# A fused scan, mixture-of-experts and Fourier-mixing kernel: the last scatters are freed from the early rows' load, and three small steps change place

## The chip, the cores and the metric

The kernel runs on one core of a Trainium2 chip. The metric is the device time of one execution in microseconds, the median of several runs. Each run is one program on one core.

## The reference

```python
# 1. attention-like scan: batch 4, heads 8, length 768, head size 32, state 16
state = decay_full * state + sum_j B_j x_j * decay_from_j       # chunk by chunk
y     = (C B^T * L) x + C state * decay_to_i
# 2. mixture of experts: x = y as [4, 768, 256], 8 experts, hidden size 1024
for each token s:
    e = argmax(logits) if s == 0 or local_gate < 0.5 else the expert of token s - 1
    out[s] = softmax(logits)[e] * (relu(x[s] @ w1[e]) @ w2[e])
# 3. Fourier mixing and a channel MLP
mixed = real(fft(fft(x, axis=1), axis=2)); u = x + mixed
un = (u - mean) / sqrt(var + 1e-6)
return u + relu(un @ w_ch1) @ w_ch2
```

## The kernel before

All of it is one program on one core, with the order of the instructions on each engine written out by hand (no planner moves anything): what stands earlier in the source is earlier in its engine's queue. Each engine runs its own queue in order and meets the others at semaphores.

**Scan and routing** (`phase_a`). Six chunks of 128 positions, each in two pairs of batches, run through TensorE. For each chunk `routing` finds every token's expert and its rank within that expert; `leave` then scatters the 4 blocks of 128 rows (each 265 words) by indirect DMA from GpSimd into the DRAM buffer `xs_buf`, sorted by expert (L643). The last chunk is routed in two halves, two scatters each. Behind the fifth chunk's scatters the Sync engine already loads the first 256 rows of expert 0 as the tile `xe` (L649): the early rows, of which only those that the first five chunks filled are used. The framework's dependency tracker lets the last chunk's four scatters, which write `xs_buf`, wait until that load has landed.

**Experts** (`experts`). First the 256 early rows go through expert 0, then expert 0's remaining 128 rows, then experts 1 to 7, with the experts sorted by load. Every weight matrix is loaded as fp32 into `r` (two buffers, shared with the raw channel weights `rawc`), copied to a high part on ScalarE (L207) and subtracted to a low part on VectorE (L210). A product is three matmuls (high with high, high with low, low with high); the hidden layer is evacuated as `hh` on ScalarE (L924, or L901 and L911 for 128 rows) and `hl` on VectorE (L925, L912). Three PSUM buffers hold the hidden products. `hook(i)` is called after each of the 8 hidden blocks (i = 0 to 7) and during the second matmul (8 to 12); all side work hangs on these hooks. In this text (e, i) is hook i of expert e.

Behind `phase_a` the Sync queue holds, in this order: the rows of expert 0 past the early ones (`load_x(0)`, L1000), the rows of expert 1 (`load_x(1)`), the two weight matrices of expert 1 (`load_w(1)`, L185 and L191), the rows of expert 2.

**Side work on the hooks.** The channel MLP's weights come as 8 chunks; `prep_steps` loads one, makes it fp32 with four VectorE operations (L144 to L147), copies the high part on ScalarE (L153), and makes the low part with a subtraction and an addition (L157, L158): chunk 0 on VectorE, the others on GpSimd. Chunk 6's low part stands at (1, 11), the last hook of expert 1. `sort_rows` sorts the rows of experts 6 and 7 once more: a load of the rows into `xu`, token numbers, a count on TensorE, four scatters (L1054); the table `SORT` says how many of its steps run on which hook. Expert outputs leave by scatters of `y_tok` from GpSimd (L1075).

**Mixing and channel MLP** (`transform`). The four batches are folded and mixed (`mid`, with `stage_a`, `stage_b`), partly beside the last expert blocks, partly on the hooks of six groups of 512 rows which go through the channel MLP. `plan` lists which step of which batch runs on which hook of which group. `split_n` transposes and splits the next group's rows at hook 10.

Of the kernel before, what the change touches and what calls it, by code (L numbers as in the profile page):

```python
# [16 lines left out]
NC = S // 128  # L17
# [7 lines left out]
EARLY = 256  # L25
# [7 lines left out]
MORE = {0: 8, 1: 10}  # L33
PREP = tuple((c, (e, 6), (e, 9)) for c, e in enumerate((1, 2, 3, 4, 5)))
PREP += ((5, (NE - 2, 7), (NE - 2, 9)), (6, (1, 9), (1, 10)), (7, (NE - 2, 9), None))
SORT = {(1, 8): 2, (1, 9): 1, (1, 10): 3, (2, 8): 2, (2, 9): 1, (2, 10): 3}

FT = (
    (((0, 0),), ((0, 1),)),
# [19 lines left out]
def tile_kernel(ctx: ExitStack, tc: tile.TileContext, io):  # L59
    nc = tc.nc  # L60
    V, A, G, PE, SP = nc.vector, nc.scalar, nc.gpsimd, nc.tensor, nc.sync
# [28 lines left out]
    xe = const.tile([128, EARLY // 128, RW], FP32, name="xe")  # L90
# [10 lines left out]
    def disjoint(name, w):  # L101
        if name in groups:
            tc.declare_no_dep(w.ins, group=name, reason="the rows of a scatter are its own")
        groups.add(name)
        tc.add_to_no_dep_group(name, w.ins)
# [13 lines left out]
    def prep_steps(i, pool):  # L119
        n = 512  # L120
        w = i // 4
        q = i % 4
        if w == 0:
            src = io["wc1"][(q // 2) * 128:(q // 2) * 128 + 128, (q % 2) * n:(q % 2 + 1) * n]
            dst = [t[:, q // 2, (q % 2) * n:(q % 2 + 1) * n] for t in wch[0:2]]
            sh = [128, n]
            raw = wraw.tile([128, n, 2], I32, tag="raw", name="rawc")
            SP.dma_start(out=raw.rearrange("p f t -> p (f t)"), in_=src.bitcast(I32))
        else:
            src = io["wc2"][q * 256:q * 256 + 256, :]  # L130
            dst = [t[:, 2 * q:2 * q + 2, :] for t in wch[2:4]]
            sh = [128, 2, D]
            raw = wraw.tile([128, n, 2], I32, tag="raw", name="rawc")
            SP.dma_start(
                out=raw.rearrange("p (k d) t -> p k (d t)", k=2),
                in_=src.bitcast(I32).rearrange("(k p) d -> p k d", p=128),
            )
            dst = [t.rearrange("p k d -> p (k d)") for t in dst]
        yield
        hw, lw = raw[:, :, 1], raw[:, :, 0]  # L140
        v = pool.tile([128, n], I32, tag="cv", name="cv")
        e = pool.tile([128, n], I32, tag="ce_", name="ce_")
        r = pool.tile([128, n], FP32, tag="cr", name="cr", bufs=1)
        V.tensor_scalar(out=e, in0=hw, scalar1=3, scalar2=0x3FFFFFF8, op0=ALU.logical_shift_left, op1=ALU.bitwise_and)  # L144
        V.scalar_tensor_tensor(out=v, in0=hw, scalar=-0x40000000, in1=e, op0=ALU.bitwise_and, op1=ALU.bitwise_or)
        V.tensor_scalar(out=e, in0=v, scalar1=-0x800000, scalar2=None, op0=ALU.bitwise_and)
        V.scalar_tensor_tensor(  # L147
            out=r, in0=lw.bitcast(mybir.dt.uint32), scalar=2.0 ** -52, in1=e.bitcast(FP32), op0=ALU.mult, op1=ALU.mult
        )
        vf = v.bitcast(FP32)  # L150
        if i == 6:
            yield
        A.activation(out=dst[0], in_=vf, func=ACTF.Copy)  # L153
        yield
        ef = e.bitcast(FP32)
        eng = G if i else V
        eng.tensor_tensor(out=ef, in0=vf, in1=dst[0], op=ALU.subtract)  # L157
        eng.tensor_tensor(out=dst[1], in0=ef, in1=r, op=ALU.add)  # L158
        yield

# [84 lines left out]
    def phase_a():  # L245
        with ExitStack() as st:
# [281 lines left out]
            def routing(c, b0, nb):  # L528
# [112 lines left out]
                def leave(bb):  # L641
                    for b in bb:
                        w = G.indirect_dma_start(  # L643
                            out=xs_buf, out_offset=bass.IndirectOffsetOnAxis(ap=si[:, b:b + 1], axis=0),
                            in_=x1n[:, b0 + b, 0:RW], in_offset=None, bounds_check=NE * NTOK - 1, oob_is_err=False,
                        )
                        disjoint("xs", w)
                    if c + 2 == NC and bb[-1] + 1 == nb:
                        SP.dma_start(out=xe, in_=xs_buf[0:EARLY, :].rearrange("(t p) r -> p t r", p=128))  # L649

                for b in range(0, nb, 2):
                    scq.append((leave, range(b, b + 2), now[0]))
# [332 lines left out]
    def load_x(pools, e, xn=None):  # L985

        n = -(-CAPS[e] // 128) * 128
        if xn is not None:
            src = xs_buf.rearrange("(e t) r -> e t r", e=NE)[bass.ds(expert(e), 1), 0:n, :]
            SP.dma_start(out=xn[:, 0:n // 128], in_=src.rearrange("o (t p) r -> p (o t) r", p=128))  # L990
            return xn
        xn = pools[0].tile([128, 4, RW], FP32, tag="xn", name="xn", bufs=3)
        if e in SORTED:
            src = xs_part[e][0:n, :].rearrange("(t p) r -> p t r", p=128)
        elif e:
            src = xs_buf.rearrange("(e t) r -> e t r", e=NE)[bass.ds(expert(e), 1), 0:n, :]
            src = src.rearrange("o (t p) r -> p (o t) r", p=128)
        else:
            src = xs_buf[bass.ds(expert(0), n), :].rearrange("(t p) r -> p t r", p=128)
        SP.dma_start(out=xn[:, 0:n // 128], in_=src)  # L1000
        return xn
# [139 lines left out]
    def experts():  # L1141

        nonlocal ws
        od = order(sm)
        for _ in range(3):
            next(od)
        xn = load_x(pools, 0)
        xn1 = load_x(pools, 1)
        keep_clock(ps2, 4)
        early = split_t((xp, pst), lambda t, d: xe[:, t, 137 * d:137 * d + 128], n=EARLY)  # L1150
        for _ in ws:
            pass
        nxt, nr, srt, chunk = None, None, [], {}

        def first(i):
            nonlocal nxt, ws
            if 0 < i < 4:
                next(od)
            if i == 0:
                ws = load_w(1)  # L1160
            if i == 6:
                past(out_e, cc("rid")[:, 0:2], nfirst.to_broadcast([128, 2]))
                tokens(ids_e, xe, out_e, 2)
            if i == 8:
                nxt = split_x(pools, xn, out_of[:, 0, :], CAPS[0])

        moe_expert(pools, 0, xe, ids_e, early, first, n=EARLY)
        last = NE - 1
        for e in range(NE):
            cur = (xn, *nxt)  # L1170
            more = e < last
            if more:
                xn = xn1
            if e + 2 < NE:
                xn1 = load_x(pools, e + 2)

            def hook(i):
                nonlocal nxt, ws, nr
                if (e, i) in ((1, 0), (2, 4)):
                    srt[:] = [sort_rows(pools, SORTED[e - 1])]  # L1180
                    next(srt[0])
                for _ in range(SORT.get((e, i), 0)):
                    next(srt[0])
                if (e, i) == (1, 9):
                    sq = sm.tile([128, 1], FP32, tag="sq", name="sq", bufs=1)
                    A.activation(out=sq, in_=ident[:, 0:1], func=ACTF.Sqrt)
                if (e, i) == (4, 8):
                    nr = rounds(sm)
                    next(nr)
                if (e, i) == (4, 10):  # L1190
                    nr = next(nr)
                at = AT.get(e, (2, 3, 4, 5, 8, 8))
                for _ in range(at.count(i) if more else 0):
                    next(ws, None)
                for c, x, y in PREP:
                    if (e, i) == x:
                        chunk[c] = prep_steps(c, sm)
                        next(chunk[c])
                    if (e, i) == y:
                        next(chunk[c])  # L1200
                        if c != 6:
                            next(chunk[c])
                if (e, i) == (1, 11):
                    next(chunk[6])
                    next(chunk[6])
                if more and (e, i) == (e, MORE.get(e, 9)):
                    next(ws, None)
                    ws = load_w(e + 2) if e + 2 < NE else None
                if i == 7 and more:
                    nxt = split_x(pools, xn, out_of[:, e + 1, :], CAP if e + 1 == last - 1 else CAPS[e + 1])  # L1210
            if e < last - 1:
                moe_expert(pools, e, *cur, hook, n=CAPS[e])
                wt.pop(e)
            elif more:
                moe_expert(pools, e, *cur, hook, n=LEAD[e][1])
                most = cur
        return (most, cur, chunk[7]), nr
# [50 lines left out]
    def transform(lead):  # L1268
# [303 lines left out]
        def turn(i):  # L1572
# [39 lines left out]
        plan = {  # L1612
# [3 lines left out]
        }  # L1616
        for g, b in ((2, 2), (3, 3)):
            for k, v in (
# [136 lines left out]
```

## Time and profile before

| | |
|---|---|
| Time, median of 3 runs | 424.89 us (423.1 to 426.29) |
| The profiled execution's own time | 426.76 us |
| Its span, first to last instruction | 425.0 us |
| Mean granted TensorE clock | 0.996 |
| TensorE matmul busy | 402.1 us (95%) |
| TensorE weight load busy | 353.8 us (83%) |
| VectorE busy | 281.8 us (66%) |
| ScalarE busy | 188.3 us (44%) |
| GpSimd busy | 147.7 us (35%) |

The span is what lies between the first and the last instruction of the profiled execution; its own time is 1.76 us longer. Busy times are sums over an engine's instructions. The granted clock is 1 at 2.4 GHz and 0.5 at 1.2 GHz. An engine's idle time stands in front of the instruction that ended it, with the instruction or DMA that released it.

### The profile page before, as it was taken

How to read it: one execution, taken by the hardware profiler on the slowest of the kernel's cores; microseconds unless marked ns; L12 is line 12 of the kernel's file. 1: busy time of each engine (PE TensorE's matmuls, PEld its weight loads, DVE VectorE, ACT ScalarE, POOL GpSimd, SP SyncE). 2: the span in 40 equal slices, each digit the busy share in tenths (PEclk: the TensorE clock that was granted, in tenths of full speed). 3: DMA queues.
4: the chain of work that ended last, by engine and by line, in shares of the span. 5: the costliest groups of instructions: out<-in, count | busy, mean ns of one | idle time of the engine just before them, and what ended most of it. 6: DMA issues, size and time to landing. Idle time of an engine off the chain costs nothing.

```text
span 425.0 us, 8313 instructions
## 1 busy us (share of the span) xinstructions
PE 402.1 (95%) x3113; PEld 353.8 (83%) x3113; DVE 281.8 (66%) x770; ACT 188.3 (44%) x409; POOL 147.7 (35%) x206
## 2 busy tenths in 40 slices
PE   8898898788799999999999999999999999999995
PEld 4576566568689989999998998798898998989885
DVE  4678878873577897676865668875576685743431
ACT  3355465523656546474675425423324344331220
POOL 1264876641001717533253606325402713200000
PEclk9999999999899999999999999999999999999999
DMA  8798454224782957586663410452113010000101
GB/s 278 245 325 279 133 173 140 78 77 148 235 280 93 261 182 238 165 260 219 168 225 99 135 56 28 139 184 56 56 39 87 15 39 0 28 25 14 37 15 42
DMA packets 34089, 56.26 MB, mean 132 GB/s; under 512 B 3318, under 2 KB 23063, under 8 KB 34040
## 3 DMA queue, kind: packets, MB, share of 16 engines
q1 hardware_dynamic: 30328, 46.82, 34.7%
q0 software_dynamic: 3200, 8.54, 5.7%
q8 instruction: 26, 0.43, 0.4%
q10 hardware_dynamic: 512, 0.28, 0.2%
q14 instruction: 23, 0.19, 0.1%
HBM read 42.60 MB, written 13.17 MB: 131 GB/s over the span
## 4 chain that ended last, share of the span: by engine, by line
PE 74%; DVE 12%; ACT 6%; DMA 5%; issue 2%; POOL 0%; SPq 0%; ACTq 0%; DVEq 0%
PE mm L918 25%; PE mm L960 20%; PE mm L936 9%; PE tl L522 3%; DMA r<-in_w_dram 3%; PE tp L979 2%; PE f L1371 2%; DVE mt L446 2%; PE g L438 2%; PE mb L286 2%; PE yb L469 1%; DVE w1l L210 1%; DVE hl L925 1%; ACT w1h L207 1%; ACT x1t L476 1%
## 5 line engine op out<-in xcount | busy, mean ns | idle before, releaser
L925 DVE SCALAR_TENSOR_TENSOR hl<-mm,hh 128x512 fp32r<-128x512 f32 (+7 forms) x112 | 65.9, 593 | 48.2 <-ACT hh L924 47.9
L924 ACT ACTIVATE hh<-mm 128x512 fp32r<-128x512 f32 (+7 forms) x112 | 57.5, 521 | 72.6 <-PE mm L918 72.6
L960 PE MATMUL mm<-c2h,hh 128*128 128x256 f32 x192 | 54.4, 283 | 0.0
L960 PE MATMUL mm<-c2h,hl 128*128 128x256 f32 x192 | 53.8, 280 | 0.1
L960 PE MATMUL mm<-c2l,hh 128*128 128x256 f32 x192 | 53.6, 279 | 0.0
L918 PE MATMUL mm<-xh,w1h 128*128 128x288 f32 (+6 forms) x128 | 41.9, 335 | 1.8 <-DVE hl L925 1.4
L1075 POOL DMA_INDIRECT y_tok<-y,ids x26 | 26.9, 1034 | 45.3 <-ACT y L1074 23.3
L918 PE MATMUL mm<-xh,w1l 128*128 128x288 f32 (+6 forms) x128 | 40.5, 323 | 0.0
L918 PE MATMUL mm<-xh,c1h 128*128 128x512 f32 x96 | 38.8, 404 | 0.1
L918 PE MATMUL mm<-xh,c1l 128*128 128x512 f32 x96 | 38.0, 396 | 0.0
L960 PEld LDWEIGHTS mm<-c2h,hl 128*128 128x128 f32 x192 | 36.1, 188 | 0.3 <-DVE hl L925 0.3
L960 PEld LDWEIGHTS mm<-c2l,hh 128*128 128x128 f32 x192 | 36.1, 188 | 0.1
L960 PEld LDWEIGHTS mm<-c2h,hh 128*128 128x128 f32 x192 | 36.1, 188 | 0.1
L446 DVE TENSOR_TENSOR mt<-g,ca 128x512 f32<-128x512 f32 x48 | 31.4, 677 | 4.8 <-PE g L438 4.7
L918 PE MATMUL mm<-xl,w1h 128*128 128x288 f32 (+6 forms) x128 | 31.2, 324 | 0.0
L210 DVE TENSOR_TENSOR w1l<-r,w1h 128x512 fp32r<-128x512 f32 x32 | 24.3, 763 | 10.0 <-ACT w1h L207 9.8
L918 PE MATMUL mm<-xl,c1h 128*128 128x512 f32 x96 | 30.1, 395 | 0.0
L643 POOL DMA_INDIRECT xs_buf<-scr,si x24 | 24.5, 1021 | 13.3 <-DVE who L852 5.0
L918 PEld LDWEIGHTS mm<-xh,w1h 128*128 128x128 f32 x128 | 24.0, 188 | 4.6 <-DVE hl L925 2.9
L960 PE MATMUL mm<-w2h,hh 128*128 128x256 f32 (+1 forms) x96 | 27.4, 293 | 0.2 <-ACT hh L911 0.2
L1511 DVE SCALAR_TENSOR_TENSOR o<-mm,ve,home 128x256 f32<-128x256 f32 x24 | 11.6, 483 | 23.7 <-PE mm L960 23.6
L960 PE MATMUL mm<-w2l,hh 128*128 128x256 f32 (+1 forms) x96 | 26.6, 285 | 0.0
(337 smaller groups left out, 981.6 us busy)
## 6 DMA issues: line engine op xcount, KB each, us to landing
r<-in_w_dram SPq DMA_DIRECT2D x16, 1024.0 KB
rawc<-in_wc_dram SPq DMA_DIRECT2D x8, 512.0 KB
out_dram<-o SPq DMA_DIRECT2D x24, 128.0 KB
home<-y_tok SPq DMA_DIRECT2D x3, 768.0 KB
xs_buf<-scr SPq DMA_DIRECT2D x8, 265.0 KB
c1h<-in_x_dram SPq DMA_DIRECT2D x4, 512.0 KB
c2h<-in_bt_dram SPq DMA_DIRECT2D x6, 256.0 KB
c2l<-in_bn_dram SPq DMA_DIRECT2D x6, 256.0 KB
```

The lines of the kernel that those rows point to most:

```text
L210: V.tensor_tensor(out=l_[:, x:y], in0=r_[:, x:y], in1=h[:, x:y], op=ALU.subtract)
L286: PE.matmul(out=ps[:, 0:w], lhsT=wrm[:, 0:128], rhs=wrm[:, 0:w], start=True, stop=True)
L446: V.tensor_tensor(out=m[:, :, 2 * q:2 * q + 2, :], in0=gp[q], in1=cc("cmask").unsqueeze(1).unsqueeze(1).to_broadcast([128, 2, 2, 128]), op ...
L522: PE.matmul(out=tl[:, 128 * g:128 * g + 137], lhsT=x1t[:, g, u, :], rhs=ca[:, o:o + 137], start=(g == 0), stop=(g == 1), skip_group_check= ...
L643: w = G.indirect_dma_start(out=xs_buf, out_offset=bass.IndirectOffsetOnAxis(ap=si[:, b:b + 1], axis=0), in_=x1n[:, b0 + b, 0:RW], in_offse ...
L918: PE.matmul(out=ps[:, 0:n], lhsT=w[:, d, f * 128:(f + 1) * 128], rhs=x[:, d, 0:n], start=(k == 0), stop=(k == 5))
L924: A.activation(out=hf, in_=ps[:, 0:n], func=ACTF.Relu)
L925: V.scalar_tensor_tensor(out=hl[:, f, 0:n], in0=ps[:, 0:n], scalar=0.0, in1=hf, op0=ALU.max, op1=ALU.subtract)
L936: PE.matmul(out=ps[:, 0:n], lhsT=w[:, f, 128 * d:128 * d + 128], rhs=h[:, f, 0:n], start=(k == 0), stop=(k == 23),)
L960: PE.matmul(out=ps[0:m, :], lhsT=h[:, f, t * 128:t * 128 + m], rhs=w[:, f, :], start=(k == 0), stop=(k == 23))
L1075: w = G.indirect_dma_start(out=y_tok, out_offset=bass.IndirectOffsetOnAxis(ap=ids[0:m, t:t + 1], axis=0), in_=y[0:m, :], in_offset=None, b ...
L1511: V.scalar_tensor_tensor(out=o, in0=ps, scalar=st_[b]["rs"][:, k:k + 1], in1=st_[b]["u"][:, k].rearrange("p t d -> p (t d)"), op0=ALU.mult ...
```

## The change

Four things change.

- The four scatters of the last chunk are declared independent of the load of the early rows: they no longer wait for it. The rows which they write lie behind those that the load's users read.
- `load_w(1)` is called before the early rows' transposes instead of at hook 0 of the early rows. It still follows `load_x(0)` and `load_x(1)`.
- Chunk 6's low part goes to VectorE and is cut in two steps: the high part's copy stays at (1, 11), the subtraction stands at (2, 0) and the addition at (2, 1). The steps of expert 7's sort at (2, 8), (2, 9) and (2, 10) move one hook on, each.
- The last of batch 1's four mixing blocks (`stage_b` with its residual rows) moves from hook 10 of group 0 to its hook 11.

```diff
-SORT = {(1, 8): 2, (1, 9): 1, (1, 10): 3, (2, 8): 2, (2, 9): 1, (2, 10): 3}
+SORT = {(1, 8): 2, (1, 9): 1, (1, 10): 3, (2, 9): 2, (2, 10): 1, (2, 11): 3}
...
-        eng = G if i else V
+        eng = V if i in (0, 6) else G
         eng.tensor_tensor(out=ef, in0=vf, in1=dst[0], op=ALU.subtract)
+        if i == 6:
+            yield
         eng.tensor_tensor(out=dst[1], in0=ef, in1=r, op=ALU.add)
...
                         disjoint("xs", w)
+                        if c + 1 == NC:
+                            tc.declare_no_dep(w.ins, group="xe", reason="ranks from the early count on; the load's rows past it are not used")
                     if c + 2 == NC and bb[-1] + 1 == nb:
-                        SP.dma_start(out=xe, in_=xs_buf[0:EARLY, :].rearrange("(t p) r -> p t r", p=128))
+                        w = SP.dma_start(out=xe, in_=xs_buf[0:EARLY, :].rearrange("(t p) r -> p t r", p=128))
+                        tc.add_to_no_dep_group("xe", w.ins)
...
         xn1 = load_x(pools, 1)
+        w1 = load_w(1)
         keep_clock(ps2, 4)
...
             if i == 0:
-                ws = load_w(1)
+                ws = w1
...
-                if (e, i) == (1, 11):
-                    next(chunk[6])
+                if (e, i) in ((1, 11), (2, 0), (2, 1)):
                     next(chunk[6])
...
-            (0, 10): ((1, 2, 2),), (1, 8): ((1, 2, 5),), (1, 9): ((1, 2, 1),),
+            (0, 10): ((1, 2, 1),), (0, 11): ((1, 2, 1),), (1, 8): ((1, 2, 5),), (1, 9): ((1, 2, 1),),
```

## Rows read from the trace of the kernel before

**Rows 1.** TensorE timeline: pauses; start us, us, engine, line, op [idle before <-releaser].
```profile
102.54 0.44 PE L979 MATMUL tp<-ca,xn 128*128 128x128 f32 x2 [1.10 <-DMA xn<-xs_buf]
...
110.47 1.15 PE L908 MATMUL tp<-ca,hr 128*128 128x128 f32 x8 [1.89 <-ACT hr L901]
...
112.54 0.69 PE L979 MATMUL tp<-ca,xn 128*128 128x128 f32 x2 [0.34 <-DVE hl L912]
...
149.74 0.47 PE L918 MATMUL mm<-xh,w1h 128*128 128x448 f32 x1 [0.69 <-DVE hl L925]
...
187.65 0.43 PE L918 MATMUL mm<-xh,w1h 128*128 128x352 f32 x1 [0.38 <-DVE hl L925]
...
291.27 0.49 PE L1429 MATMUL mix<-fb,home 128*128 128x129 f32 x2 [0.53 <-DVE xl L982]
```

**Rows 2.** GpSimd timeline around the last scatters, same columns.
```profile
81.39 0.98 POOL L643 DMA_INDIRECT xs_buf<-scr,si  x1 [1.96 <-DVE er L577]
...
91.75 0.98 POOL L643 DMA_INDIRECT xs_buf<-scr,si  x1 [4.98 <-DVE who L852]
...
95.61 0.98 POOL L643 DMA_INDIRECT xs_buf<-scr,si  x1 [0.30 <-issue]
```

**Rows 3.** VectorE timeline around the last ranks, same columns.
```profile
80.45 0.16 DVE L636 SCALAR_TENSOR_TENSOR si<-f__1197,rk 128x4 int32<-128x4 f32 x1
...
88.10 0.16 DVE L636 SCALAR_TENSOR_TENSOR si<-f__1287,rk 128x2 int32<-128x2 f32 x1
...
89.13 0.16 DVE L636 SCALAR_TENSOR_TENSOR si<-f__1346,rk 128x2 int32<-128x2 f32 x1
```

**Rows 4.** Sync's DMA issues, 85 to 105 us.
```profile
88.14 0.38 SPq L649 DMA_DIRECT2D xe<-xs_buf  x1
100.36 1.32 SPq L1000 DMA_DIRECT2D xn<-xs_buf  x2
```

**Rows 5.** Chain that ended last: start us, us, what.
```profile
101.86 6.91 DMA r<-in_w_dram
...
140.33 5.05 PE mm L918 x24
```

**Rows 6.** ScalarE timeline, 104 to 114 us.
```profile
108.88 1.06 ACT L207 ACTIVATE w1h<-r 128x1024 fp32r<-128x1024 f32 x1 [2.58 <-DMA r<-in_w_dram]
109.84 1.07 ACT L901 ACTIVATE hr<-mm 128x512 f32<-128x512 f32 x2
```

**Rows 7.** By stretch: us, busy of five engines, granted clock, DMA share, GB/s.
```profile
90.00:90.50 0.50, 0.50 (x4) 0.45 (x3) 0.42 (x3) 0.00 (x0) 0.00 (x0) 1.00 0.60 208
92.50:93.00 0.50, 0.50 (x4) 0.50 (x5) 0.50 (x2) 0.20 (x1) 0.23 (x1) 1.00 0.00 0
110.00:112.00 2.00, 1.53 (x12) 1.28 (x12) 1.50 (x3) 1.74 (x4) 0.00 (x0) 0.94 1.10 362
112.00:114.00 2.00, 1.66 (x8) 1.46 (x8) 1.85 (x4) 1.97 (x4) 0.00 (x0) 0.50 0.19 66
114.00:118.00 4.00, 4.00 (x28) 3.87 (x27) 3.99 (x6) 2.63 (x4) 0.00 (x0) 0.85 0.52 163
```

**Rows 8.** TensorE weight loads at the early rows.
```profile
91.28 0.58 PEld L979 LDWEIGHTS tp<-ca,xe 128*128 128x128 f32 x4
```

**Rows 9.** VectorE timeline, 136 to 156 us.
```profile
137.92 0.69 DVE L157 TENSOR_TENSOR ce__1932<-cv,c1h 128x512 f32<-128x512 f32 x1
...
146.93 2.22 DVE L210 TENSOR_TENSOR w1l<-r,w1h 128x512 fp32r<-128x512 f32 x1 [0.32 <-ACT w1h L207]
...
155.38 0.16 DVE L1004 SCALAR_TENSOR_TENSOR tk<-xu,out_of 128x4 int32<-128x4 int32 x1 [0.74 <-DMA xu<-xs_buf]
```

**Rows 10.** GpSimd timeline, 140 to 170 us.
```profile
147.28 1.31 POOL L157 TENSOR_TENSOR ce__1998<-cv,c2h 128x512 f32<-128x512 f32 x1
148.67 1.62 POOL L158 TENSOR_TENSOR c2l<-ce__1998,cr 128x512 fp32r<-128x512 f32 x1
```

**Rows 11.** VectorE timeline, 170 to 178 us.
```profile
176.73 0.16 DVE L1004 SCALAR_TENSOR_TENSOR ids<-xn,out_of 128x3 int32<-128x3 int32 x1 [4.01 <-DMA y_tok<-y,ids]
```

## The prediction

> **What bounds the kernel now.** I read the page first: TensorE is busy 402.1 of 425.0 us, so at most some 23 us can come from its pauses, and a change that touches only VectorE, GpSimd and transfers can gain only there or in TensorE's clock. So I listed TensorE's pauses in its timeline. Behind the scan there are few: 1.10 us in front of the transposes of expert 0's remaining rows, 1.89 us in front of the hidden layer's transposes of the same 128 rows, 0.34 us behind that, and later 0.69, 0.38 and 0.53 us [rows 1]. The view by stretch adds a loss that no pause shows: from about 112 to 115.5 us, right behind the 1.89 us pause, the granted clock is at 0.5, which is 1.2 GHz [rows 7]. Everywhere else behind the scan TensorE works without a pause over 0.4 us, so a microsecond saved in front of it should reach the end unless another chain comes late.
>
> Next I asked what ends the two large pauses. The 1.10 us end with the landing of expert 0's rows, issued by Sync at 100.36 [rows 1, 4]. The 1.89 us end with the evacuation of the hidden layer on ScalarE, at 109.84, which could have run earlier, but stands in ScalarE's queue behind the high part of expert 1's first weights, and that waited 2.58 us for its transfer [rows 6]. The transfer was issued at 101.86, right behind the row loads, and took 6.91 us [rows 5]. So both pauses hang on when Sync gets past the row loads, and these wait for the last of four scatters, started at 95.61 [rows 2]. GpSimd started the first of the four at 91.75 after 4.98 us idle, although its ranks were written at 88.10 and those of the last two at 89.13 [rows 2, 3]. What it waited for is the early rows' load, issued at 88.14 [rows 4]; the releaser that the view names is a VectorE operation whose result no scatter reads.
>
> **The scatters without the wait.** The first scatter's ranks are ready at 88.10 + 0.16 = 88.26. How soon GpSimd then starts is bounded by two rows: a scatter that follows another starts 0.30 us behind it [rows 2], while the fifth chunk's first scatter started at 81.39, 0.78 us behind ranks that ended at 80.45 + 0.16 [rows 2, 3]. That gives 88.56 to 89.04 instead of 91.75, a lead of 2.7 to 3.2 us; I take 3.0, as the fifth chunk's case is the same code. The four start 1.29 us apart ((95.61 - 91.75) / 3), and the ranks of the last two are there in time, so the last starts at 92.6 and the row loads at 97.4, all 3.0 earlier.
>
> The 1.10 us pause: TensorE wanted the rows at 101.44. They landed about 2.2 us behind their issue (100.36 to 102.54), so they are there at 99.6. The pause is gone: **-1.10**, with 1.8 us in hand.
>
> The 1.89 us pause: the weights land at 108.77 - 3.0 = 105.8. The copy starts at 105.9, the first evacuation 0.96 behind it (109.84 - 108.88, [rows 6]) at 106.85, and its 0.6 us end at 107.45. TensorE arrives at 108.58 - 1.10 = 107.48. So the first half is just in time; the second half's evacuation can only start when TensorE has ended its product, and costs it some 0.15 us of waiting between two sets of four transposes that run back to back now. **-1.75**; with a lead of 2.7 it is -1.45, with the whole pause gone -1.89. The 0.34 us pause is a round trip through ScalarE and VectorE (transposes out, `hh`, `hl`, PSUM free) and stays.
>
> The clock: the stretches lose 2 x 0.06 + 2 x 0.50 + 4 x 0.15 = 1.72 us of full-speed time [rows 7]; the 0.34 us pause lies in them, and a pause loses nothing to the clock, so 1.55 us. The clock fell behind pauses of 1.10 and 1.89 us, and what I expect to be left of these is 0.15 us. **-1.55**, bounds 0 and -1.7. The Trainium skill ("TensorE: Matmul & The Clock Gate", Part 1: The HAM clock gate) says that the chip watches windows which run freely, not from the kernel's start, so that the same kernel can change its clock at other points from run to run; the one trace here can't show that.
>
> Two costs stand against it. The first scatters now share the transfer engines with the end of the early rows' load, which moves its bytes until 90.5 at a DMA share of 0.60 [rows 7]. TensorE takes up these rows at 91.28, out of padding products, without waiting [rows 8]. The scatter started at 91.75 had moved no bytes by 93.0 [rows 7], 1.25 us on, so at 88.6 the first one's bytes meet only the last half microsecond; half of a share of 0.6 gives 0.3 us at most. I take **+0.1**, bounds 0 and 0.35. And expert 1's weights come 3.0 us earlier while TensorE comes 4.4 earlier, so what hangs on them (low parts, the buffers they free, expert 2's load) has 1.4 us less in hand. TensorE did not wait there before; I take **+0.3**, bounds 0 and 1.4.
>
> The Trainium skill speaks against the earlier scatters in one point ("SBUF — State Buffer", Who interferes with whom): GpSimd can't write the descriptors of a scatter while VectorE runs a copy or scalar operation in a two-port mode. Beside the earlier scatters VectorE runs the expert order's small operations, of which some are of that kind. By that rule each could hold a scatter by its own 0.15 to 0.17 us, which would take some 0.6 us off the lead and leave it at 2.4 us; no row here shows it, since GpSimd was idle there.
>
> **`load_w(1)` earlier in the source.** Sync holds the same loads in the same order, with nothing else between, and the last readers of its two buffers, the low parts of expert 0's weights, stand ahead of both places. It costs and gives **0**.
>
> **Chunk 6 on VectorE.** GpSimd loses a subtraction of 1.31 and an addition of 1.62 us [rows 10]. Beside them VectorE's low part of expert 3's weights took 2.22 us, against 0.69 for an operation of the same size without GpSimd beside it [rows 9]. Behind it stands the `hl` for which TensorE paused 0.69 us [rows 1]. VectorE gets back 1.5 us and pays 2 x 0.69 = 1.38 us, at hooks (2, 0) and (2, 1), ahead of the low part. There `hl` of blocks 1 and 2 come later by 0.7 and 1.4 us. TensorE needs the first block's buffer three blocks on; with 5.05 / 4 = 1.26 us for each [rows 5] I count about 0.3 us to spare, for the later ones too. So the 0.69 us pause goes, with little in hand: **-0.6**, bounds +0.5 and -0.69. Nobody waits for GpSimd's freed time: its next work is chunk 1's, seven hooks on.
>
> **Expert 7's sort one hook later.** At (2, 8) VectorE stood 0.74 us in front of the sorted rows' load, and the low parts of expert 3's second weights stood behind it [rows 9]. One hook later the load has landed. The four scatters at the end of the sort stand behind chunk 1's two GpSimd operations in both versions, and these start when VectorE has ended its own part, now some 0.7 us earlier; so the scatters do not move back although their hook does. Behind them on GpSimd are expert 2's output scatters, for which VectorE later waits 4.01 us [rows 11], and that delay leads over the next weights to the 0.38 us pause [rows 1]. **-0.2**, bounds +0.4 (the hook decides after all) and -0.38. TensorE's two small count products also move; their operands are ready a half product before.
>
> **The mixing block later.** The 0.53 us pause stands before the mixing block's first product, which needs a transpose buffer that VectorE's `xl` has to free [rows 1]. A hook later, behind the 24 products of a row tile, it is free. The block's additions on GpSimd and VectorE come one row tile later, ahead of the next group's first `hl`, and so do the gathers for batch 2 behind them on GpSimd, whose users stand in the next group. **-0.5**, bounds 0 and -0.53.
>
> **Sum.** -1.10 - 1.75 - 1.55 + 0.1 + 0.3 - 0.6 - 0.2 - 0.5 = -5.3 us. The profiled execution took 426.76, its span 425.0; 1.76 us lie around it. It would take 421.5. It was 1.87 us over the median of 424.89, which the change is compared with, so the forecast is 424.9 - 5.3 = **419.6 us**, with 417.9 to 421 as its own range. 1% of this kernel, 4.25 us, is about what a measurement of it can tell from no change.
>
> **Rivals.**
> - *The clock stays low.* The shortened pauses, or new ones near 108 us, still let the clock fall for as long: 419.6 + 1.55 = 421.1. For it: I don't know which of the two pauses brought it down. Against it: pauses of 0.38 us and less elsewhere leave it at 1. Chance 0.10. The Trainium skill's rule of the freely running window, named above, would let this happen in some runs and not in others.
> - *The weights take over.* Row loads and weights share the transfer engines, which the stretch at 110 us shows full (share 1.10, [rows 7]). If the weights gain only 1.5 of the 3.0 us, about 1.3 us of the second pause remains and the clock falls: 419.6 + 1.3 + 1.55 = 422.4. Against it: the same transfers stand in the same order behind each other, only earlier. Chance 0.10.
> - *The wait stays.* If the declaration doesn't reach what really holds the scatters, only the three small steps are left: 424.9 - 1.3 = 423.6. For it: the view names another releaser. Chance 0.06.
> - *Slower: the early rows come late.* If the load of the early rows lands only behind all four scatters, at about 96.6 instead of 91.3, TensorE starts the experts 5.3 us later, and its pause pulls the clock down for another 1.7 us; against a gain of 5.3 that is 424.9 + 1.7 = 426.6. It decides from a delay of about 5 us. For it: they share 16 engines. Against it: the load is issued before them and its bytes are nearly all moved at 90. Chance 0.04.
>
> The forecast has 0.70. Range: 417.8 to 422.6 takes in the forecast's own bounds and the first two rivals. Faster by over 1% (below 420.6): most of the forecast's case and a little of the first rival, 0.65; within 1%: 0.32; slower: 0.03.
>
> **What the changed profile would show.** The last chunk's first scatter starts at 88.6 to 89.0, the row loads at 97.2 to 97.7, expert 1's first weights land at about 105.8; no pause before the transposes at 101.4, at most 0.3 us before the hidden transposes, and a clock of 1 throughout. Chunk 6's two operations stand on VectorE with 0.69 us each, no low part beside them takes over 0.7, and the pauses at hooks (2, 7) and (0, 10) are gone. Wrong it would be by a start of the scatters near 91, by a pause before 92 on the early rows, or by a new TensorE pause in experts 2 to 4 in which weights or `hl` come late.

## The result, and the profile after

The changed kernel takes **420.55 us**, the median of 6 runs (420.16 to 421.25); the kernel before took 424.83 in 6 runs beside it (423.1 to 427.8). The medians differ by 4.3 us, and the recorded ratio is 0.9889 [0.9863, 0.9914]: faster by 1.1%, between 3.7 and 5.8 us. Where some runs of a kernel stand apart in a slower state, the ratios of this document leave them out and the medians are of all runs, so that a ratio can differ from the quotient of the two medians. The time lies inside the predicted 417.8 to 422.6, and 0.95 us above the forecast of 419.6. The profiled execution took 420.29, 0.26 under its median.

Where the 4.3 us came from is read in the order of the prediction, first GpSimd's timeline of the kernel after (start us, us, engine, line, operation, idle before and its releaser):

```profile
89.09 0.98 POOL L645 DMA_INDIRECT xs_buf<-scr,si  x1 [2.26 <-issue]
90.37 0.99 POOL L645 DMA_INDIRECT xs_buf<-scr,si  x1 [0.31 <-DVE pl L848]
91.67 0.98 POOL L645 DMA_INDIRECT xs_buf<-scr,si  x1 [0.30 <-DVE who L857]
92.95 0.98 POOL L645 DMA_INDIRECT xs_buf<-scr,si  x1 [0.30 <-issue]
```

Sync's DMA issues of the kernel after:

```profile
96.21 1.32 SPq L1005 DMA_DIRECT2D xn<-xs_buf  x2
97.71 0.70 SPq L187 DMA_DIRECT2D r<-in_w_dram  x1
```

The last chunk's first scatter starts at 89.09 and the last at 92.95, 2.66 us earlier than in [rows 2]. The row loads follow at 96.21, though, 4.15 us earlier than in [rows 4]: from the last scatter's start to the issue of the row loads it took 4.75 us before and takes 3.26 now. The weights are issued at 97.71 instead of 101.86 [rows 5].

ScalarE's timeline of the kernel after, at the copy of expert 1's first weights:

```profile
104.98 1.06 ACT L209 ACTIVATE w1h<-r 128x1024 fp32r<-128x1024 f32 x1
105.95 0.59 ACT L906 ACTIVATE hr<-mm 128x512 f32<-128x512 f32 x1
107.34 0.60 ACT L906 ACTIVATE hr<-mm 128x512 f32<-128x512 f32 x1 [0.80 <-PE mm L901]
```

TensorE's timeline of the kernel after, the hidden transposes, the pause that answers to the one at 187.65 in [rows 1], and the mixing block's first product:

```profile
107.14 0.60 PE L913 MATMUL tp<-ca,hr 128*128 128x128 f32 x4
107.99 0.66 PE L913 MATMUL tp<-ca,hr 128*128 128x128 f32 x4 [0.25 <-ACT hr L906]
...
181.95 0.43 PE L923 MATMUL mm<-xh,w1h 128*128 128x352 f32 x1 [0.22 <-DVE hl L930]
...
287.70 0.38 PE L1434 MATMUL mix<-fb,home 128*128 128x129 f32 x2
```

The copy no longer waits for its transfer, and the first half's evacuation stands right behind it and is done when TensorE arrives at 107.14. What is left of the 1.89 us is 0.25 us between two sets of four transposes. The pauses of 1.10, 0.34, 0.69 and 0.53 us in [rows 1] have no row any more.

VectorE's timeline of the kernel after; the first row is a step of the expert order beside the freed scatters:

```profile
91.03 0.33 DVE L857 TENSOR_SCALAR who<-pl 128x7 int32<-128x7 f32 x1
...
139.19 0.68 DVE L157 TENSOR_TENSOR ce__1998<-cv,c2h 128x512 f32<-128x512 f32 x1
...
140.32 0.68 DVE L160 TENSOR_TENSOR c2l<-ce__1998,cr 128x512 fp32r<-128x512 f32 x1
...
142.39 0.69 DVE L212 TENSOR_TENSOR w1l<-r,w1h 128x512 fp32r<-128x512 f32 x1 [0.31 <-ACT w1h L209]
...
151.18 0.16 DVE L1009 SCALAR_TENSOR_TENSOR tk<-xu,out_of 128x4 int32<-128x4 int32 x1 [0.57 <-DMA xu<-xs_buf]
```

Chunk 6's two operations cost 0.68 us each, and the low part of expert 3's weights takes 0.69 instead of 2.22 us [rows 9]. The sort's first step waits 0.57 us for its rows, where it waited 0.74.

To place the gain I cut the experts' time at three products that start in both kernels. The view by stretch is read in pairs: length in us, busy time and count of TensorE, its weight loads, VectorE, ScalarE and GpSimd, then granted clock, DMA share and GB/s. Before, from expert 0's first product to expert 1's, on to a second product at 189.54, and from another one at 221.93 to the channel MLP's product at 294.79, behind the mixing block's first:

```profile
92.47:117.21 24.74, 21.41 (x151) 19.77 (x152) 12.39 (x33) 11.69 (x23) 5.16 (x6) 0.93 0.56 180
117.21:189.54 72.33, 71.25 (x452) 66.81 (x451) 54.53 (x106) 41.25 (x73) 28.74 (x26) 1.00 0.68 215
...
221.93:294.79 72.86, 71.41 (x509) 66.03 (x509) 51.91 (x147) 31.05 (x73) 26.68 (x39) 1.00 0.29 97
```

The same stretches of the kernel after, from product to product:

```profile
92.53:112.67 20.14, 19.77 (x151) 18.61 (x152) 10.82 (x31) 11.18 (x23) 3.06 (x4) 1.00 0.58 192
112.67:183.83 71.16, 70.94 (x451) 66.93 (x451) 55.08 (x110) 41.53 (x74) 26.72 (x24) 1.00 0.70 223
...
216.20:288.30 72.10, 71.19 (x509) 65.97 (x509) 51.88 (x146) 30.61 (x71) 25.22 (x36) 1.00 0.30 98
```

The first stretch is 4.60 us shorter (24.74 to 20.14), the second 1.17, the third 0.76; the rest differs by under 0.1. So the profiled spans differ by 6.5 us (425.0 to 418.5) where the medians differ by 4.3. Most of that difference sits in the first stretch, whose clock was 0.93 before and is 1.00 now: 24.74 x 0.07 is about 1.7 us that the profiled execution of before lost to the clock, and that execution was 1.87 us over its median.

### The profile page after: what moved, and what is told of

Same layout as the page of the kernel before. It is cut to its first block, busy times and chain, and to the rows that moved or that the text cites. A ratio compares the mean times of both kernels' runs of the same rounds, so it can differ in the third digit from the quotient of the medians.

```text
span 418.5 us, 8310 instructions
## 1 busy us (share of the span) xinstructions
PE 400.0 (96%) x3113; PEld 352.7 (84%) x3113; DVE 281.1 (67%) x772; ACT 188.1 (45%) x409; POOL 145.2 (35%) x204
## 4 chain that ended last, share of the span: by engine, by line
PE 79%; DVE 11%; ACT 5%; DMA 2%; issue 2%; POOL 0%; ACTq 0%; DVEq 0%
PE mm L923 27%; PE mm L965 21%; PE mm L941 9%; PE tl L524 3%; PE tp L984 2%; PE f L1376 2%; DVE mt L448 2%; PE g L440 2%; PE mb L288 2%; PE yb L471 2%; PE mm L901 1%; DMA r<-in_w_dram 1%; ACT x1t L478 1%; DVE hl L930 1%; PE yb L460 1%
## 5 line engine op out<-in xcount | busy, mean ns | idle before, releaser
L645 POOL DMA_INDIRECT xs_buf<-scr,si x24 | 24.5, 1023 | 10.6 <-issue 6.7
L212 DVE TENSOR_TENSOR w1l<-r,w1h 128x512 fp32r<-128x512 f32 x32 | 22.2, 699 | 7.2 <-ACT w1h L209 7.0
```

The lines of the kernel that those rows point to most:

```text
L212: V.tensor_tensor(out=l_[:, x:y], in0=r_[:, x:y], in1=h[:, x:y], op=ALU.subtract)
L645: w = G.indirect_dma_start(out=xs_buf, out_offset=bass.IndirectOffsetOnAxis(ap=si[:, b:b + 1], axis=0), in_=x1n[:, b0 + b, 0:RW], in_offse ...
```

## The experiments

The theory: both large pauses were TensorE being early for rows and weights that hang on the scatters, and the small steps take away VectorE's contention and two waits. The rivals: the gain is the clock's, which the pauses brought down; or the weights' place in the source does it. Twelve runs in three series follow, and the record names another chip for each series (0, 10 and 14). In the first and the third the kernel before took about 8 us more (medians 433.9 of 35 runs and 433.1 of 31) than in the second (424.9 of 23). In every profiled execution of these two series TensorE was late behind the scan, and in all but one its mean granted clock lay between 0.971 and 0.982. The one, `c1_before`, took 431.28 us at 0.995, so the clock is not the whole of the 8 us; what is, and whether it goes with the chip, is not shown. Each kernel is compared only with the runs of before in its own series.

### First series: the parts one at a time

**The kernel before once more**, unchanged, as the series' own trace.

> The kernel before, once more. Theory A (the prediction's sum): every execution has the 1.10 and 1.89 us pauses and the stretch at half clock, so times lie within 1 us of each other near 425, with a mean granted clock of 0.996 in each. Rival B (the clock falls in some executions only): times spread over 2 us or more, those with a clock of 1.000 near 423.3, those with 0.996 or less near 425 or above; then the clock term of 1.55 us counts in part of the executions, and the median gains less than the profiled one.

434.15 us, ratio 1.0019 [0.9979, 1.0058], a time that neither theory had. The view by stretch of this run of before shows the end of the scan:

```profile
53.00:60.00 7.00, 5.30 (x37) 4.11 (x37) 3.64 (x7) 2.83 (x8) 6.22 (x10) 0.76 0.35 138
60.00:82.00 22.00, 17.89 (x264) 13.33 (x264) 18.12 (x54) 11.61 (x29) 12.04 (x18) 1.00 0.43 129
82.00:99.00 17.00, 16.50 (x75) 9.92 (x75) 11.34 (x57) 5.03 (x15) 6.42 (x9) 0.50 0.20 64
```

From 82 to 99 us the clock is at 0.50, with TensorE busy for 16.50 of 17 us. TensorE's and GpSimd's timelines of the same run:

```profile
54.58 1.18 PE L522 MATMUL tl<-ca,x1t 128*128 128x137 f32 x4 [2.38 <-ACT x1t L476]
...
103.12 0.39 PE L918 MATMUL mm<-xh,w1h 128*128 128x256 f32 x1 [0.38 <-issue]
...
118.57 0.66 PE L908 MATMUL tp<-ca,hr 128*128 128x128 f32 x4 [0.25 <-ACT hr L901]
...
98.08 0.98 POOL L643 DMA_INDIRECT xs_buf<-scr,si  x1 [5.70 <-DVE scr L626]
```

TensorE waited 2.38 us at 54.58, and 1.48 us at 80.56, for `x1t`. ScalarE's copy that makes `x1t` had itself waited: 2.00 us the first time, for a releaser that the trace only calls `remote`, and 1.28 us the second time, for TensorE's `mb` (L560). What held the scan up stays open. Expert 0's first product starts at 103.12, 10.6 us later than in the profile before (92.47), the last chunk's first scatter only 6.3 us later (98.08; 91.75 in [rows 2]). Its ranks were written from 97.14 to 97.30, so it follows them by 0.78 us, as the fifth chunk's scatter does in [rows 2, 3]: the early rows' load holds up nothing here. Neither the 1.10 nor the 1.89 us pause is there; the second stands at the 0.25 us that the kernel after has.

**Only the scatters freed.** The edit is the two declarations:

```diff
+                        if c + 1 == NC:
+                            tc.declare_no_dep(w.ins, group="xe", reason="ranks from the early count on; the load's rows past it are not used")
-                        SP.dma_start(out=xe, ...)
+                        w = SP.dma_start(out=xe, ...)
+                        tc.add_to_no_dep_group("xe", w.ins)
```

> Only the last chunk's scatters are freed. Theory A: -1.10 - 1.75 - 1.55 + 0.4 = -4.0 us, 420.8, with no pause before the transposes at 101.3 and 0.25 us before the hidden ones; the pauses of 0.69 and 0.53 us further on remain. Rival B (the gain is in the small steps and the weights' call): no more than -2 us. Rival C (the weights' call is needed for it): expert 1's weights are issued where they were, so a pause of over 1 us stays before the hidden transposes.

432.45 us, ratio 0.9958 [0.992, 0.9996]. In this series TensorE came late by itself and there were no large pauses to remove; the interval (0.2 to 3.5 us less) decides nothing more.

**Only the three small steps**: chunk 6's low part, the sort, the mixing.

```diff
-SORT = {(1, 8): 2, (1, 9): 1, (1, 10): 3, (2, 8): 2, (2, 9): 1, (2, 10): 3}
+SORT = {(1, 8): 2, (1, 9): 1, (1, 10): 3, (2, 9): 2, (2, 10): 1, (2, 11): 3}
-        eng = G if i else V
+        eng = V if i in (0, 6) else G
-                if (e, i) == (1, 11):
+                if (e, i) in ((1, 11), (2, 0), (2, 1)):
-            (0, 10): ((1, 2, 2),), (1, 8): ((1, 2, 5),), (1, 9): ((1, 2, 1),),
+            (0, 10): ((1, 2, 1),), (0, 11): ((1, 2, 1),), (1, 8): ((1, 2, 5),), (1, 9): ((1, 2, 1),),
```

> Only the three small steps: chunk 6's low part on VectorE, the sort and the mixing block one hook later. Theory A: -0.6 - 0.2 - 0.5 = -1.3 us, 423.5, with the two large pauses as before. Rival B (the small steps only help once TensorE comes earlier, or lose as much in hooks 2, 0 and 2, 1): between -0.3 and +0.5 us.

432.35 us, ratio 0.9977 [0.9939, 1.0014]. The pauses at chunk 6 and at the mixing block are gone from the trace; the time alone can't tell that from nothing.

**Only the weights' load moved up in the source.**

```diff
+        w1 = load_w(1)
         keep_clock(ps2, 4)
-                ws = load_w(1)
+                ws = w1
```

> Only the call of expert 1's weight loads stands earlier. Theory A: Sync's queue is the same, so 0 us, within 0.5, with the weights issued at 101.9 as before. Rival B: the weights are issued earlier than 101.5 and the second pause shrinks, -0.5 us or more.

433.87 us, ratio 0.9982 [0.9944, 1.002]. Sync issues the row loads at 102.95 and the weights at 104.46 and 105.10, in the same order and at the same distance as in [rows 4, 5]. The move changes nothing in Sync's queue, and the time (2.4 us less to 0.9 us more) shows no effect.

### Second series: the two pauses and the clock

**The kernel after once more.**

> The changed kernel once more, beside the kernel before. In the first series of experiments the clock fell in the scan already, TensorE came about 3 us later to the expert phase and the kernel before had no pause of 1.10 and 1.89 us left to win. Theory A (the gain of the scatters hangs on when TensorE leaves the scan): where the scan runs at full clock, -4 to -5 us; where its tail runs at half clock, -1 to -2.5 us, from the small steps alone. Rival B (the gain is the same whatever the clock): -4 to -5 us in both.

420.55 us, ratio 0.9907 [0.9875, 0.9938], beside 424.94 for the kernel before (23 runs): -4.4 us by the medians, 2.6 to 5.3 us by the ratio. The runs of before in this series show a mean clock of 0.999 (median), those of after 0.997 to 1.000: this gain holds next to nothing of the clock. Two of the 23 runs of before have a mean clock of 0.993 and 0.994, and they are the two slowest (427.06 and 427.52 us). The second stretch of this execution:

```profile
112.30:184.03 71.73, 70.96 (x452) 66.94 (x452) 55.09 (x110) 41.50 (x74) 26.37 (x24) 1.00 0.68 220
```

It is 0.57 us longer than in the first execution of the same kernel (71.16): so much can one stretch differ from execution to execution.

**Only the scatters freed**, the same edit as above.

> Only the scatters are freed, once more. Theory A: with a full clock in the scan -4.0 us, with pauses of 0.69 and 0.53 us left further on; with a half clock in its tail within 1 us of no change, since there is no pause to win in front of expert 1. Rival B: between -1.5 and -2.5 us in either case.

423.15 us, ratio 0.9969 [0.9938, 0.9999]. GpSimd's, Sync's and TensorE's timelines of this kernel, and its second stretch:

```profile
93.37 0.98 POOL L643 DMA_INDIRECT xs_buf<-scr,si  x1 [0.31 <-issue]
...
96.62 1.32 SPq L1003 DMA_DIRECT2D xn<-xs_buf  x2
...
108.41 0.66 PE L911 MATMUL tp<-ca,hr 128*128 128x128 f32 x4 [0.25 <-ACT hr L904]
145.66 0.47 PE L921 MATMUL mm<-xh,w1h 128*128 128x448 f32 x1 [0.69 <-DVE hl L928]
179.78 0.43 PE L921 MATMUL mm<-xh,w1h 128*128 128x352 f32 x1 [0.44 <-DVE hl L928]
...
287.61 0.49 PE L1432 MATMUL mix<-fb,home 128*128 128x129 f32 x2 [0.53 <-DVE xl L985]
...
113.12:185.89 72.77, 71.53 (x452) 66.87 (x451) 55.75 (x108) 41.27 (x74) 29.29 (x26) 1.00 0.69 218
```

Both large pauses are gone with this one edit, and the pauses of the three small steps are all there. Its first stretch (92.95 to 113.12, from the chain of waits) is 20.17 us long, against 20.14 after: the scatters' edit does the whole of it. Its second is 72.77 us, 0.44 longer than before and 1.6 longer than after. In the chain of waits it stands behind expert 2's output scatters, which took 4.00 us to land, where the chain of before has 3.20; as 0.44 is less than the 0.57 between two executions of the kernel after, it is not shown to be a cost of the edit. Its third (218.27 to 291.12) is 72.85, as long as before. The trace is that of theory A. The time, 1.8 us less, is rival B's: theory A's 4.0 us counted 1.55 us of clock, which nearly all runs of before in this series had not lost.

**Padding in the place of the second pause.** In the kernel before, idle products that nobody reads fill the time before expert 0's hidden transposes. If the 1.89 us pause made the clock fall, filling it keeps the clock.

```diff
             flush()
+            if e == 0:
+                keep_clock(ps2, 4)
```

> The kernel before, with 4 padding products (2.0 us at full clock) in TensorE's queue in front of the hidden transposes of expert 0's remaining rows, where it paused 1.89 us. It adds work that no output uses. Theory A (the pause pulls the clock down): the clock stays at 1.0 behind it and the kernel is faster by up to 1.5 us, although TensorE does more. Rival B (the clock falls for another reason, or by the 1.10 us pause alone): the stretch at half clock remains, and the time is the same or up to 1 us longer.

425.5 us, ratio 1.002 [0.9994, 1.0046]. Behind the padding the clock is 1.00 (108 to 116 us), and the first pause in front of it is still 1.21 us long. That was meant to settle what brings the clock down, but 21 of the 23 runs of before in this series kept a mean clock of 0.997 to 1.000 too, so it settles nothing.

**TensorE later on purpose.** Twelve padding products instead of four in front of the early rows in the kernel before: TensorE is delayed, the scatters still wait.

```diff
-        keep_clock(ps2, 4)
+        keep_clock(ps2, 12)
```

> The kernel before, with 12 padding products instead of 4 behind the scan, so that TensorE comes 3.9 us later to the early rows while scatters and loads stay where they are. It adds work that no output uses. Theory A (the two pauses only exist because TensorE is early, so a delay of up to about 3 us is free): both pauses are gone, the clock stays up, and the time is within 1 us of the kernel before. Rival B (the pauses follow from something that moves with TensorE): the pauses remain and the time is 3.5 us longer or more.

426.27 us, ratio 1.0032 [1.0008, 1.0055]. GpSimd's, Sync's and TensorE's timelines:

```profile
95.55 0.98 POOL L643 DMA_INDIRECT xs_buf<-scr,si  x1 [0.30 <-issue]
...
98.86 2.04 SPq L1000 DMA_DIRECT2D xn<-xs_buf  x2
...
96.16 0.39 PE L918 MATMUL mm<-xh,w1h 128*128 128x256 f32 x1 [0.38 <-ACT xh L981]
...
111.62 0.66 PE L908 MATMUL tp<-ca,hr 128*128 128x128 f32 x4 [0.25 <-ACT hr L901]
```

Expert 0 starts at 96.16, 3.7 us later, and the whole costs only 1.3 us (0.3 to 2.3 by the ratio). The scatters start when they did before, and yet both pauses are gone. The row loads were issued 1.50 us earlier than in [rows 4] and the weights 0.78 us (at 101.08), but that is not what removed the pauses: 3.7 us later, TensorE would have wanted the rows at 105.1 (101.44 + 3.7), which landed at 102.54 before, and the hidden layer at 111.2 (107.48 + 3.7), which it got at 110.47 [rows 1]. So the pauses were TensorE being too early for the rows and weights; of 3.7 us of plain delay 2.4 came back.

### Third series: what stayed open

**The kernel before a third time.**

> The kernel before, once more, for a profile of a common execution. The runs of before beside the second series lie near 424.9 with a mean clock of 0.998 to 1.000, which leaves no room for 3.4 us at half clock. Theory A (the profiled execution of before was one of a few in which the clock fell behind the pauses): the pauses of about 1.1 and 1.9 us are there, the clock behind them is 1.00, and expert 1's first product comes 24.7 - 1.5 = 23.2 us after that of the early rows, instead of 24.7. Rival B (the fall is usual): the clock falls as in the first profile.

431.84 us, ratio 0.9968 [0.9933, 1.0003]. GpSimd's, Sync's and TensorE's timelines and the view by stretch of this run of before:

```profile
102.09 0.98 POOL L643 DMA_INDIRECT xs_buf<-scr,si  x1 [0.30 <-issue]
...
106.64 1.32 SPq L1000 DMA_DIRECT2D xn<-xs_buf  x2
...
81.47 0.73 PE L522 MATMUL tl<-ca,x1t 128*128 128x137 f32 x4 [3.01 <-ACT x1t L476]
...
108.86 0.44 PE L979 MATMUL tp<-ca,xn 128*128 128x128 f32 x2 [0.26 <-DMA xn<-xs_buf]
...
116.41 1.15 PE L908 MATMUL tp<-ca,hr 128*128 128x128 f32 x8 [1.52 <-ACT hr L901]
...
114.00:118.00 4.00, 2.48 (x16) 1.66 (x14) 1.56 (x3) 2.92 (x5) 0.00 (x0) 1.00 1.09 372
118.00:120.00 2.00, 1.51 (x13) 1.52 (x14) 1.85 (x4) 2.00 (x5) 0.00 (x0) 1.00 0.30 106
```

Here is the second pause, 1.52 us, with a clock of 1.00 behind it, where [rows 7] had 0.50 and 0.85; of the first pause 0.26 us is left. A pause at this place is followed by a low clock in one execution and not in another. It is no exact repetition, though, as both pauses are shorter than the 1.10 and 1.89 us of [rows 1].

**The expert order's last steps later.** From the last scatter's start to the row loads it took 4.75 us before and 3.26 after, which I hadn't expected. In the kernel before, VectorE's small steps of the expert order run beside that scatter; here they go behind it.

```diff
-            if 0 < i < 4:
+            if 4 < i < 8:
                 next(od)
```

> The kernel before, with the last three steps of the expert order (VectorE) at hooks 5 to 7 of the early rows instead of 1 to 3, so that they run behind the last scatter and not beside it. Where these steps ran beside the last scatter, the row loads were issued 4.75 us behind its start, elsewhere 3.3 us. Theory A (VectorE's steps hold up the scatter): 3.3 us, row loads and weights 1.4 us earlier, the 1.1 us pause gone and the 1.9 us pause down to about 1.5: -1.4 us. Rival B (the lag is by chance or from elsewhere): 4.7 us as before, no change in time.

432.27 us, ratio 1.0064 [1.0006, 1.0122]: no gain is shown. The lag is 3.32 us (103.12 to 106.44). But the clock had fallen in the scan and TensorE came late (first product at 102.63), where the unchanged kernel also shows 3.24 (101.93 to 105.17 in the first series). The run doesn't tell the two apart.

**Chunk 6's low part back on GpSimd, at the new hooks** of the kernel after.

```diff
-        eng = V if i in (0, 6) else G
+        eng = G if i else V
```

> The changed kernel, with chunk 6's low part on GpSimd again, but at the new hooks (2, 0) and (2, 1). Theory A (what counts is that GpSimd and VectorE don't read at once): low parts of expert 3's first weights beside it take 1.3 to 2.2 us on VectorE instead of 0.7, the 0.7 us pause at hook (2, 7) is back: +0.7 us on the changed kernel. Rival B (what counts is the hook): no such pause, within 0.3 us of the changed kernel.

431.66 us, ratio to before 0.997 [0.9926, 1.0015]. VectorE's, GpSimd's and TensorE's timelines:

```profile
151.35 2.23 DVE L212 TENSOR_TENSOR w1l<-r,w1h 128x512 fp32r<-128x512 f32 x1 [0.32 <-ACT w1h L209]
...
154.04 1.22 DVE L212 TENSOR_TENSOR w1l<-r,w1h 128x512 fp32r<-128x512 f32 x1
...
151.72 1.31 POOL L157 TENSOR_TENSOR ce__1998<-cv,c2h 128x512 f32<-128x512 f32 x1
153.10 1.61 POOL L160 TENSOR_TENSOR c2l<-ce__1998,cr 128x512 fp32r<-128x512 f32 x1
...
154.17 0.47 PE L923 MATMUL mm<-xh,w1h 128*128 128x448 f32 x1 [0.71 <-DVE hl L930]
```

With the low part on GpSimd, VectorE's low part takes 2.23 and 1.22 instead of 0.69 us, and TensorE's pause is back at 0.71. The engine decides, not the hook. The Trainium skill ("SBUF — State Buffer", Who interferes with whom) says that a VectorE instruction with two SBUF inputs contends with a GpSimd instruction that reads SBUF; both are of that kind, and the trace agrees.

**The sort back at its old hooks** in the kernel after.

```diff
-SORT = {(1, 8): 2, (1, 9): 1, (1, 10): 3, (2, 9): 2, (2, 10): 1, (2, 11): 3}
+SORT = {(1, 8): 2, (1, 9): 1, (1, 10): 3, (2, 8): 2, (2, 9): 1, (2, 10): 3}
```

> The changed kernel, with expert 7's sort at hooks (2, 8) to (2, 10) again. Theory A (the prediction's 0.2 us): VectorE stands about 0.7 us for the rows at (2, 8), the scatters of the sort start about 0.7 us later, and the pause in expert 4 grows by 0.2 to 0.7 us: +0.2 to +0.7 us. Rival B (chunk 1's raw weights hold the same place, or the scatters' hook decides): no change, or up to 0.4 us faster.

433.99 us, ratio to before 0.9993 [0.9952, 1.0034]. Sync's, VectorE's and TensorE's timelines:

```profile
158.73 0.37 SPq L995 DMA_DIRECT2D xu<-xs_buf  x1
...
163.13 0.16 DVE L1009 SCALAR_TENSOR_TENSOR tk<-xu,out_of 128x4 int32<-128x4 int32 x1 [3.23 <-DMA xu<-xs_buf]
...
163.85 0.36 PE L1032 MATMUL ps<-ahead,cb 128*128 128x5 f32 x2 [1.20 <-DVE ahead L1027]
```

VectorE stands 3.23 us for the sorted rows, where it stood 0.74 in [rows 9], and TensorE waits 1.20 us for its count. Counted from expert 0's first product, the load was issued 54.9 us on, and 54.7 in `s1_before`; TensorE wanted its count 58.8 us on, and 59.5 in `s1_before`. So TensorE reaches the hook earlier, and the rows don't come earlier. In this execution the old place takes more (1.20 us) than the 0.69 us pause that chunk 6's move removed. The time doesn't price it, since no run of the kernel after stands in this series.

## Why the prediction was right, and where it was not

**The scatters: right.** They started 0.78 us behind the ranks (88.15 + 0.16 to 89.09), as the fifth chunk's do; the lead is 2.66 us where I took 3.0. They stand 1.28 to 1.30 us apart, as before, so the small VectorE operations beside them did not hold them, as the rule of the Trainium skill ("SBUF — State Buffer", Who interferes with whom) could have had it. The contention is on the other side: `who` took VectorE 0.33 us at 91.03 and ended with the scatter of 90.37, where it took 0.17 before. In all six runs in which it meets a scatter it took 0.33 to 0.41 us and ended within 0.02 us of the scatter's end; in the other eight it took 0.17.

**The row loads: the mechanism right, the lead too small.** I kept 4.75 us from the last scatter's start to the row loads; it fell to 3.26, so rows and weights came 4.15 us earlier, not 3.0. The lag is 3.2 to 3.4 us in the eleven runs in which the last steps of the expert order run on VectorE behind the last scatter's own 0.98 us, and 4.55 to 5.1 in the three in which they run beside it (before, `b3_pad`, `c1_before`). `b4_late` narrows it: its scatters start within 0.06 us of those of [rows 2], and with everything behind the scan 3.7 us later the lag is 3.31. So what runs beside the last scatter goes together with the lag; that it is these steps is not shown.

**The pauses: right.** -1.10 came in full, -1.75 as -1.64, and the 0.34 us that I had left standing went too: 3.08 us of the first stretch's 4.60. The rest, 1.52, is the clock.

**The clock: the step that failed.** "The clock fell behind pauses of 1.10 and 1.89 us [...] **-1.55**" is right for the execution that was profiled, and the forecast takes it off the median, which it is no part of. That execution stood 1.87 us over the median; I used that number to convert one into the other and did not ask whether the fall was what made it slow. In `c1_before` a pause of 1.52 us at the same place leaves the clock at 1.00, and in the second series the gain is 4.4 us although the runs of before have a mean clock of 0.999. The Trainium skill ("TensorE: Matmul & The Clock Gate", Part 1: The HAM clock gate) says that the clock's windows run freely, so that the same kernel can change its clock at other points from run to run; these runs agree with that. Without the term the forecast would have been 424.9 - 3.75 = 421.15. What brings the clock down in some executions and not in others stays open.

**What made up for it.** The +0.1 for the shared transfers did not come: the early rows were taken up at 91.55 without a wait. The +0.3 for weights less in hand is not shown either: the 0.44 us of `b2_scatter` is no more than one stretch differs between executions. Counted by the profiled stretches the whole is 3.08 + 1.17 + 0.76 = 5.0 us without the clock, where the forecast without the clock had 3.75: the 0.34 us pause less 0.11 of the second, the two costs of 0.4 that did not come, and 0.63 more from the small steps. That these nearly make up for the 1.55 us of the clock is luck. The medians say 4.3 and 4.4 us, and 5.0 lies inside both intervals (3.7 to 5.8 and 2.6 to 5.3). The scatters alone are worth 2.6 to 3.1 us by the stretches, with or without the 0.44, and 1.8 by the medians (0.0 to 2.6 by the ratio).

**Chunk 6 (-0.6), the sort (-0.2), the mixing block (-0.5): right in kind, too small.** Both pauses are gone, and `c3_pool6` shows that the one at chunk 6 comes with GpSimd's work beside VectorE. From `b2_scatter` to `a1_after` the three are worth (72.77 - 71.73) + (72.85 - 72.11) = 1.8 us, and 2.4 to the first execution of after, where I had 1.3. The mixing block's part, 0.74, exceeds its pause by 0.2. For the sort I wrote that one hook later the load has landed: it has not, VectorE still waits 0.57 us. And the sort was under-priced: with the low parts done sooner its old place costs 1.20 us (`c4_no_sort`), a wait that I priced only by what it was in the kernel before. What is left near 182 us, 0.22 in one execution of after and 0.77 in the other, hangs on a weights transfer that took 5.10 and 5.67 us in their chains.

**`load_w(1)`: 0, as predicted** (`s4_weights`).

**The rivals.** The wait did not stay, the weights did not take over, the early rows came in time, and the clock stayed at 1.00 behind what is left of the pauses. A case that came up in the first and third series was not among them: TensorE and the last ranks come late for a reason of their own, so that the early rows' load holds nothing up. Freeing the scatters gave 0.2 to 3.5 us there (`s2_scatter`), with no large pause in the trace of before to remove. `c1_before` came 6.6 us late as well, but with the scatters still held (4.85 us idle) and 1.78 us of pauses.

## What to carry to other kernels

When the profiled execution stands above its median, look for what is in it and not in its neighbours, and take such a term off that execution alone. What freeing a wait is worth depends on how early its consumer comes: delaying the consumer on purpose (`b4_late`) is a cheap way to measure it. A step that looks worth 0.2 us in the old kernel can cost or give more behind another gain (1.20 us in `c4_no_sort`), so price it with that gain in place.

## What the runs showed of the hardware that was not expected

- One program on one core took 425 us in one series and 433 to 434 in two others, the three on three chips. In `s1_before` the clock was at 0.50 from 82 to 99 us, with TensorE busy for 16.50 us of that; the pause in front of the fall was 1.48 us. In `c1_before` a pause of 3.01 us, at 81.47, left the clock at 1.00 (81 to 100 us).
- VectorE's `who` (128x7) was held up by a scatter beside it and ended with it: 0.33 to 0.41 us in six runs, 0.17 in the eight where it met none.
- In the profile before, the transfers behind the last scatter moved 144 GB/s from 97 to 98 us, 8 from 98 to 99 and 0 from 99 to 100; the chain has that scatter landing at 99.69, 4.09 us after its start, and the row loads were issued at 100.36. After the change it was 136 GB/s from 94.5 to 95.5 us and 0 from 95.5 to 96.5, with the row loads at 96.21.
